# Projection split into halves on POOL, the second half of w2 staged through SP, and smaller landing margins in the planner of a fused hash-attention and maxout-FFN kernel

## The chip, the core and the metric

The kernel runs on one core of a Trainium2 chip. The metric is the device time in microseconds. A core has these engines: PE (matmul), DVE (vector), ACT (activation), POOL (GpSimd) and SP, which here only issues DMAs. Each engine works through its own queue in order, and waits at an instruction until what that instruction needs has been signalled. Everything queued behind it waits too.

## The reference

```python
q_bits = (np.einsum('bhsd,dk->bhsk', q, proj) > 0)         # batch 4, heads 8, seq 768, dim 64; 6 bits
k_bits = (np.einsum('bhsd,dk->bhsk', k, proj) > 0)
mask = q_bucket[:, :, :, None] == k_bucket[:, :, None, :]  # bucket: the 6 bits as a number
scores = np.where(mask, scale * q @ k.T, -1e9)
attn = softmax(scores)                                      # over the keys
x = (attn @ v).transpose(0, 2, 1, 3).reshape(3072, 512)
h = np.maximum(np.maximum(x @ w1, x @ w2), x @ w3)          # 512 -> 768
out = h @ w_out                                             # 768 -> 512, float32
```

## The kernel before

**The data path.** The work goes by pairs of heads, written (b, pr): batch b of 4, pair pr of 4. For each pair q and k are loaded in float32 and split into two float16 halves, a high part (split_h, L266 on ACT or L268 on DVE) and a residual (split_r, L273 on DVE). Both halves lie beside each other in a tile `s`. It is transposed into the operand tile `T`, by PE matmuls (L292) and copies (evac_T, L202 on ACT or L204 on DVE) for the first six pairs, and by a transposing DMA on SP (xbar, L282) for the others. `hash_mm` (L310, L312) multiplies T by the projection, which is held in the tile `PAB` as a float16 high part and a residual, both times 1024. The sign of the sum gives the bits (hash_bits, L330 and L332). The bits then replace the residual rows of T, so that the score matmul (L395) adds a large number for each bit that agrees, and the exponential (L401 on ACT) of anything else is zero. For the first pair the bits are written into `s` and transposed again. For all others they are transposed (bps, L339), copied (bt, L344), written to DRAM by SP (bit_out, L349, `dr<-bt`) and read back into T by SP (bit_in, L352, `T<-dr`). This is called the bounce below.

A unit is one score group (two L395 matmuls), one exponential on ACT and one attend group (six L413 matmuls). 192 units make the attention, six to a block; a block is normalized on DVE (L430, L436, L449). For rows whose bucket is empty the mean of v is added: from batch 1 on POOL sums v over its chunks (vsum, L363, L365, L366) and PE multiplies the sum by ones (mean_mm, L376, tile `svp`). In batch 0 PE does it from `vone` alone (L373).

The FFN takes half a batch of rows at a time: L478 matmuls by w1, w2 and w3, maxima on DVE (L487), L496 matmuls by w_out, copies and stores. Its float16 weights stay on chip. Each of w1, w2 and w3 comes in two halves of columns, named (half, i) with i = 0, 1, 2. By default a half is one DMA from POOL that converts on the way (`load_w`, L541). The halves in `plain`, and w_out ("o"), go another way: SP loads them in float32 in pieces (`stage_w`, L663) into one of two buffers `ws`, and POOL casts each piece (`cast_w`, L204).

**The order.** Nothing runs in program order of the loops. Every step is a task with the engines that may take it and their durations, a priority, dependences and buffers to take and give. `Plan.run` simulates the engines and a single queue of transfers (`xfer`), picks by priority what is free to start, and emits each instruction in that order into the engine queues. A DMA counts as landed when its transfer has passed that queue, plus POST = 1.2, plus the task's own `pad`: the landing margin. The queues of the hardware are fixed by this; a wait there costs what it costs. PE gets small filler matmuls (L771) until the first score, when it has nothing else.

The lines that the change touches: `make_p` (L231 to L239) and its task `mp` (L536) build PAB from `p32`. The key of the PSUM bank of `hash_mm` (L300, L315, L328) carries no head. The pads stand at the xbar task (L620) and at bit_in (L630). `plain` (L649) holds one half:

```python
    mp = add(("DVE", 0.5), -300, [add(("ACT", 0.1), -500, [], lambda e: None, lat=3.2)], make_p)
    ...
    plain = ((1, 2),)
    ...
    stage = {(0, 3): [(1, 0), (1, 1)], (1, 0): [(1, 2)], (1, 1): ["o"]}
```

`stage` says after which pair's bounce the weights are fetched: (1, 0) and (1, 1) after that of (0,3), (1, 2) after that of (1,0).

Of the kernel before, what the change touches and what calls it, by code (L numbers as in the profile page):

```python
# [10 lines left out]
AluOp = mybir.AluOpType  # L11
# [16 lines left out]
class Plan:  # L28
# [12 lines left out]
    def add(self, kinds, prio, deps, emit, **kw):  # L41
        t = Task(kinds if isinstance(kinds, list) else [kinds], prio, deps, emit, **kw)
        self.tasks.append(t)
        return t
# [89 lines left out]
def kernel(  # L134
# [12 lines left out]
    nc = tc.nc  # L147
    B, H, S, D = q.shape
    NBITS = proj.shape[1]
# [9 lines left out]
    NA = 4 * NCH  # L159
# [27 lines left out]
    op = ctx.enter_context(tc.tile_pool(name="op", bufs=OSB))  # L187
# [9 lines left out]
    add = plan.add  # L197
# [33 lines left out]
    def make_p(e):  # L231
        ph = konst.tile([D, NBITS], FP16, name="ph")
        pr32 = konst.tile([D, NBITS], FP32, name="pr32")
        nc.vector.tensor_copy(ph[:], p32[:])
        nc.vector.tensor_tensor(out=pr32[:], in0=p32[:], in1=ph[:], op=AluOp.subtract)
        for o in (0, D):
            for i, src in enumerate((ph, pr32)):
                nc.vector.tensor_scalar(out=PAB[o : o + D, NBITS * i : NBITS * (i + 1)], in0=src[:],
                                        scalar1=1024.0, scalar2=None, op0=AluOp.mult)  # L239


# [39 lines left out]
    def xbar(b, pr, e):  # L281
        nc.sync.dma_start_transpose(operand(b, pr)[:], S16[b, pr][:].rearrange("p a d -> p (a d)"))  # L282

    def bank(key, name):
        pss[key] = mm_ps.tile([P, 512], FP32, tag="mm", name=name)
        return pss[key]
# [10 lines left out]
        copy(e, operand(b, pr)[:, a0:a1, :].rearrange("p a t -> p (a t)"), p16[:, 0 : NCH * P])  # L297

    def hash_mm(b, pr, heads, e):
        hps = bank(("h", b, pr), "hps")  # L300
        summed = 4 * b + pr < 2
        K = NBITS if summed else 2 * NBITS
        for n in range(2):
            for hh in range(*heads):
                for c in range(NCH):
                    a = n * NA2 + hh * NCH + c
                    o = hps[:, a * K : (a + 1) * K]
                    if summed:
                        for i in range(2):
                            nc.tensor.matmul(o, T[b, pr][:, a, :], PAB[:, i * K : (i + 1) * K], start=i == 0, stop=i == 1)  # L310
                    else:
                        nc.tensor.matmul(o, T[b, pr][:, a, :], PAB[:], start=True, stop=True)  # L312

    def hash_bits0(pr, heads, e):
        hv = pss.pop(("h", 0, pr))[:, 0 : NA * NBITS].rearrange("p (n a k) -> p n a k", n=2, k=NBITS)  # L315
        sl = slice(heads[0] * NCH, heads[1] * NCH)
        bit = small.tile([P, 2, NA2, NBITS], FP16, tag="bit", name="bit")
        if pr:
            bits[0, pr] = bit
            nc.vector.tensor_scalar(out=bit[:], in0=hv, scalar1=0.0, scalar2=None, op0=AluOp.is_gt)  # L320
            return
        nc.vector.tensor_scalar(out=bit[:, :, sl, :], in0=hv[:, :, sl, :], scalar1=0.0, scalar2=0.5,  # L322
                                op0=AluOp.is_gt, op1=AluOp.subtract)
        nc.vector.tensor_scalar(out=S16[0, pr][:].rearrange("p (n a) d -> p n a d", n=2)[:, :, sl, D : D + NBITS],
                                in0=bit[:, :, sl, :], scalar1=2 * BIT, scalar2=None, op0=AluOp.mult)

    def hash_bits(b, pr, e):
        hv = pss.pop(("h", b, pr))[:, 0 : NA * 2 * NBITS].rearrange("p (a k) -> p a k", k=2 * NBITS)  # L328
        neg = small.tile([P, NA, NBITS], FP32, tag="neg", name="neg")
        nc.vector.tensor_scalar(out=neg[:], in0=hv[:, :, NBITS : 2 * NBITS], scalar1=-1.0, scalar2=None, op0=AluOp.mult)  # L330
        bits[b, pr] = bit = small.tile([P, 2, NA2, NBITS], FP16, tag="bit", name="bit")
        nc.vector.tensor_tensor(out=bit[:].rearrange("p n a k -> p (n a) k"), in0=hv[:, :, 0:NBITS], in1=neg[:],  # L332
                                op=AluOp.is_gt)
# [17 lines left out]
    def bit_in(b, pr, e):  # L351
        nc.sync.dma_start(T[b, pr][D : D + NBITS, :, :],  # L352
                          drs.pop((b, pr))[:].rearrange("n (a k) t -> k (n a) t", k=NBITS))
# [178 lines left out]
    for i, (n, pr, heads) in enumerate(order):  # L532
        half = heads != (0, 2)
        loads[n, 0, pr, heads] = add(("SP", 0.45), -400 + i, [], lambda e, n=n, pr=pr, heads=heads: load(n, 0, pr, heads, e),
                                     take=(n,) if heads[0] == 0 else (), xfer=0.55 if half else 1.1)
    mp = add(("DVE", 0.5), -300, [add(("ACT", 0.1), -500, [], lambda e: None, lat=3.2)], make_p)  # L536

    def load_w(i, half, e):
        w_ap = (moe_w1, moe_w2, moe_w3)[i].rearrange("(c p) f -> p c f", p=P)
# [21 lines left out]
    def prep(b, pr):  # L561
# [55 lines left out]
                                  give=("mm",)))  # L617
            both_rs += rs
        if not by_pe:
            ev = [add(("SP", 0.6), p0 + 2, both_rs, lambda e: xbar(b, pr, e), pad=4, xfer=4.6, hold=3.4, take=("T",))]  # L620
            xbars[4 * b + pr] = ev[0]
        plan.join(ev, ("s",))
        hm = add(("PE", 1.3 if 4 * b + pr < 2 else 0.67), p0 + 4, ev + [mp], lambda e: hash_mm(b, pr, (0, 2), e), take=("mm",))
# [3 lines left out]
        be = add(("DVE", 0.28), p0 + 6, [bT], lambda e: bit_evac(b, pr, e), take=("bt",), give=("mm",))  # L627
        bo = add(("SP", 0.65), p0 + 7, [be], lambda e: bit_out(b, pr, e), take=("dr",), give=("bt",), xfer=0.05,
                 after=[last_copy[0]])
        bi = add(("SP", 0.65), p0 + 7, [bo], lambda e: bit_in(b, pr, e), give=("dr",), xfer=0.25, pad=3 if 4 * b + pr > 5 else 0.0)  # L630
        bounced[b, pr] = last_copy[0] = bi
        if b == 0 and pr < NP - 1:
            for hh in range(2):
# [12 lines left out]
        t = small.tile([P, 1], FP16, tag="hold", name="hold")  # L646
        nc.gpsimd.tensor_copy(t[D : D + NBITS, :], T[b, pr][D : D + NBITS, NA - 1, P - 1 : P])

    plain = ((1, 2),)  # L649
    wst_tiles = {}  # L650

    def w_view(w, i):
# [153 lines left out]
```

The softmax here doesn't subtract the row's maximum and nothing guards it: scores larger than these inputs give would overflow.

## Time and profile before

| | before |
|---|---|
| median of 5 runs | 267.32 us (266.16 to 268.58) |
| profiled execution, its own time | 266.16 us |
| its span, first to last instruction | 264.4 us |
| PE busy | 255.6 us (97%) |
| ACT busy | 196.3 us (74%) |
| DVE busy | 174.7 us (66%) |
| POOL busy | 41.9 us (16%) |
| granted PE clock | 0.999 |

The profile holds one execution. Its times are microseconds from the start of the span; the 1.8 us between span and own time lie around it. "Busy" counts an instruction from start to end, also where matmuls overlap. Of the page, the slices show where in the span an engine worked, the chain shows what released each step of the work that ended last. In a timeline a line gives start, length, engine, source line, operation, tiles, and in brackets how long the engine had stood idle and what ended that. "SPq" and "POOLq" lines are the issue of DMAs, not the transfers.

### The profile page before, as it was taken

What the parts mean: (1) busy time and instruction counts of PE and PEld (TensorE: products, weight loads), DVE (VectorE), ACT (ScalarE), POOL (GpSimd) and SP (SyncE); (2) the same over time, 40 slices, a digit from 0 to 9 for tenths busy, and PEclk for the clock granted to TensorE, in tenths of its full rate; (3) what the DMA queues carried; (4) which work ended last, traced back from release to release, by engine and by line L of the source; (5) the groups of instructions that cost most, each with busy time, mean ns of one, the idle gap of its engine ahead of it and who ended that gap; (6) DMA issues with size and microseconds to landing.
All of it is one profiled execution on the core that took longest, in us unless ns stands there. A gap on an engine that the chain in (4) does not pass through costs nothing.

```text
span 264.4 us, 7323 instructions
## 1 busy us (share of the span) xinstructions
PE 255.6 (97%) x2992; PEld 174.0 (66%) x2992; DVE 174.7 (66%) x394; ACT 196.3 (74%) x283; POOL 41.9 (16%) x57
## 2 busy tenths in 40 slices
PE   7898899999999999999999999999999999999995
PEld 7787677767656666676666767766666656555552
DVE  4899589999748898468985795561655526255260
ACT  4799799997936889989899889989898632332322
POOL 1431054273311223003330030000000000000000
PEclk9999999999999999999999999999999999999999
DMA  6995489799997999979994995302030060120303
GB/s 206 342 277 90 135 265 267 228 230 338 218 224 253 241 255 171 236 210 207 211 246 140 219 179 103 71 14 109 12 62 0 4 179 4 40 79 0 121 0 120
DMA packets 67408, 41.69 MB, mean 158 GB/s; under 512 B 48046, under 2 KB 63662, under 8 KB 67374
## 3 DMA queue, kind: packets, MB, share of 16 engines
q1 hardware_dynamic: 64654, 39.26, 57.8%
q0 software_dynamic: 2640, 1.97, 4.8%
q8 instruction: 23, 0.38, 0.6%
q14 instruction: 11, 0.09, 0.1%
q10 hardware_dynamic: 80, 0.00, 0.0%
HBM read 25.72 MB, written 6.84 MB: 123 GB/s over the span
## 4 chain that ended last, share of the span: by engine, by line
PE 87%; ACT 5%; DMA 3%; DVE 3%; issue 1%; SPq 1%; ACTq 0%
PE ps L478 35%; PE sc L395 22%; PE av L413 12%; PE po L496 11%; ACT AT L401 4%; PE hps L312 3%; DMA q<-in_q_dram 2%; PE tps L292 1%; DMA T<-dr 1%; DVE s L268 1%; DVE s L273 1%; PE hps L310 1%; SPq L250 1%; PE bps L339 1%; ACT T L202 1%
## 5 line engine op out<-in xcount | busy, mean ns | idle before, releaser
L401 ACT ACTIVATE AT<-sc 128x768 f16<-128x768 f32 x192 | 146.2, 815 | 15.0 <-PE sc L395 12.9
L478 PE MATMUL ps<-xT,w_sb 128*128 128x384 f16 x576 | 106.3, 326 | 0.0
L395 PE MATMUL sc<-T 128*128 128x384 f16 x384 | 93.0, 325 | 2.6 <-DMA T<-dr 1.6
L487 DVE TENSOR_TENSOR ht<-ht,ps 128x384 f16<-128x384 f16 x96 | 52.9, 552 | 47.1 <-PE ps L478 44.6
L413 PEld LDWEIGHTS <-AT 128*128 128x128 f16 x1152 | 59.5, 97 | 22.6
L478 PEld LDWEIGHTS <-w_sb 128*128 128x128 f16 x576 | 52.6, 98 | 30.1
L413 PE MATMUL av<-vone,AT 128*128 128x65 f16 x1152 | 65.5, 193 | 0.0
L395 PEld LDWEIGHTS <-T 128*128 128x128 f16 x384 | 30.2, 97 | 13.2 <-DMA T<-dr 1.8
L496 PE MATMUL po<-wout_sb,ht 128*128 128x512 f16 (+1 forms) x150 | 33.6, 370 | 0.0
L202 ACT CAST ht<-ps 128x384 f16<-128x384 f32 x28 | 13.5, 480 | 26.4 <-DVE ht L487 19.1
L202 ACT COPY osb<-po 128x512 f32<-128x512 f32 (+1 forms) x24 | 13.7, 569 | 18.3 <-PE po L496 18.3
L363 POOL TENSOR_TENSOR vt<-v 128x384 f32<-128x384 f32 x12 | 13.6, 1134 | 66.4 <-DMA v<-in_v_dram 66.3
L430 DVE TENSOR_TENSOR t<-av,mv 128x390 f32<-128x390 f32 x32 | 18.0, 561 | 8.1 <-PE av L413 8.0
L496 PEld LDWEIGHTS <-ht 128*128 128x128 f16 x150 | 14.1, 98 | 13.7
L273 DVE SCALAR_TENSOR_TENSOR s<-q,s 128x384 f16<-128x384 f32 x32 | 20.2, 646 | 3.3 <-ACT s L266 3.2
L449 DVE TENSOR_TENSOR xn<-t,rr 128x384 f16<-128x384 f32 x32 | 18.7, 583 | 1.1
L273 DVE SCALAR_TENSOR_TENSOR s<-k,s 128x384 f16<-128x384 f32 x32 | 17.7, 574 | 0.4 <-ACT s L266 0.2
L204 DVE CAST ht<-ps 128x384 f16<-128x384 f32 x20 | 11.1, 556 | 10.1 <-PE ps L478 9.7
L292 PE MATMUL tps<-iden,s 128*128 128x128 f16 x168 | 13.3, 219 | 1.8 <-DVE bit L322 1.1
L292 PEld LDWEIGHTS <-s 128*128 128x128 f16 x168 | 10.3, 97 | 3.3 <-DVE s L273 2.2
L312 PEld LDWEIGHTS <-T 128*128 128x128 f16 x336 | 10.0, 96 | 1.0
L312 PE MATMUL hps<-PAB,T 128*128 128x12 f16 x336 | 10.4, 168 | 0.0
(54 smaller groups left out, 141.7 us busy)
## 6 DMA issues: line engine op xcount, KB each, us to landing
v<-in_v_dram SPq DMA_DIRECT2D x16, 384.0 KB
out_dram<-osb SPq DMA_DIRECT2D x23, 256.0 KB
q<-in_q_dram SPq DMA_DIRECT2D x15, 384.0 KB
k<-in_k_dram SPq DMA_DIRECT2D x15, 384.0 KB
w_sb<-in_moe_w_dram POOLq DMA_DIRECT2D x5, 384.0 KB, 10.9
ws<-in_moe_w_out_dram SPq DMA_DIRECT2D x3, 512.0 KB
ws<-in_moe_w_dram SPq DMA_DIRECT2D x2, 384.0 KB
dr<-bt SPq DMA_DIRECT2D x15, 36.0 KB
```

Of the source, the lines that this page charges most:

```text
L202: nc.scalar.copy(o, i)
L273: nc.vector.scalar_tensor_tensor(out=s[:, a0:a1, D : 2 * D], in0=raw_view(n, b, pr, heads), scalar=QS, in1=s[:, a0:a1, 0:D], op0=AluOp.mul ...
L292: nc.tensor.transpose(p16[:, c * P : (c + 1) * P], S16[b, pr][:, a0 + c, :], iden[:])
L312: nc.tensor.matmul(o, T[b, pr][:, a, :], PAB[:], start=True, stop=True)
L395: nc.tensor.matmul(sc[:, i, 0:HQ], t[:, NA2 + hh * NCH + 2 * j + i, :], t[:, hh * NCH + hf * CH : hh * NCH + (hf + 1) * CH, :], start=True ...
L401: nc.scalar.activation(AT[:], scs.pop(u)[:, :, 0:HQ], ActFn.Exp, bias=EXP_BIAS, scale=EXP_SCALE)
L413: nc.tensor.matmul(av[:, o : o + D + 1], AT[:, i, c * P : (c + 1) * P], vones[b % 2][:, 2 * pr + hh, 2 * j + i, 0 : D + 1], start=slot == ...
L430: nc.vector.tensor_tensor(out=t[:, :, :, 0 : D + 1], in0=av[:, :, :, 0 : D + 1], in1=mv, op=AluOp.add)
L449: nc.vector.tensor_tensor(out=xv, in0=t[:, :, :, 0:D], in1=rr[:].to_broadcast([P, 2, CH, D]), op=AluOp.mult)
L478: nc.tensor.matmul(ps[:, 0:HQ], w_sb[i][:, jc, fb * P : (fb + 1) * P], xTs[b, hf][:, jc, :], start=jc == 0, stop=jc == NJ - 1)
L487: nc.vector.tensor_tensor(out=ht[:], in0=ht[:], in1=ps[:, 0:HQ], op=AluOp.max)
L496: nc.tensor.matmul(ps[:, m0:m1], hts[b, hf, fb][:, c * P : (c + 1) * P], wout_sb[:, fb, m0:m1], start=fb == 0, stop=fb == NF - 1)
```

## The change

Four edits. `make_p` issues its six instructions on POOL, and its task is planned there with 1.5 in place of 0.5. The PSUM bank of the hash gets the first head into its key, so that the two heads of pair (0,0) may be in flight in two banks. The pads of xbar and bit_in are one unit smaller. The half (1, 1), the second half of w2, joins `plain`: SP loads it in two pieces and POOL casts them, where one POOL DMA did it before. As the planner lays out all queues from these numbers, the order on every engine changes.

```diff
     def make_p(e):
         ph = konst.tile([D, NBITS], FP16, name="ph")
         pr32 = konst.tile([D, NBITS], FP32, name="pr32")
-        nc.vector.tensor_copy(ph[:], p32[:])
-        nc.vector.tensor_tensor(out=pr32[:], in0=p32[:], in1=ph[:], op=AluOp.subtract)
+        nc.gpsimd.tensor_copy(ph[:], p32[:])
+        nc.gpsimd.tensor_tensor(out=pr32[:], in0=p32[:], in1=ph[:], op=AluOp.subtract)
         for o in (0, D):
             for i, src in enumerate((ph, pr32)):
-                nc.vector.tensor_scalar(out=PAB[o : o + D, NBITS * i : NBITS * (i + 1)], in0=src[:],
+                nc.gpsimd.tensor_scalar(out=PAB[o : o + D, NBITS * i : NBITS * (i + 1)], in0=src[:],
                                         scalar1=1024.0, scalar2=None, op0=AluOp.mult)
...
-        hps = bank(("h", b, pr), "hps")
+        hps = bank(("h", b, pr, heads[0]), "hps")
...
-        hv = pss.pop(("h", 0, pr))[:, 0 : NA * NBITS].rearrange("p (n a k) -> p n a k", n=2, k=NBITS)
+        hv = pss.pop(("h", 0, pr, heads[0]))[:, 0 : NA * NBITS].rearrange("p (n a k) -> p n a k", n=2, k=NBITS)
...
-        hv = pss.pop(("h", b, pr))[:, 0 : NA * 2 * NBITS].rearrange("p (a k) -> p a k", k=2 * NBITS)
+        hv = pss.pop(("h", b, pr, 0))[:, 0 : NA * 2 * NBITS].rearrange("p (a k) -> p a k", k=2 * NBITS)
...
-    mp = add(("DVE", 0.5), -300, [add(("ACT", 0.1), -500, [], lambda e: None, lat=3.2)], make_p)
+    mp = add(("POOL", 1.5), -300, [add(("ACT", 0.1), -500, [], lambda e: None, lat=3.2)], make_p)
...
-            ev = [add(("SP", 0.6), p0 + 2, both_rs, lambda e: xbar(b, pr, e), pad=4, xfer=4.6, hold=3.4, take=("T",))]
+            ev = [add(("SP", 0.6), p0 + 2, both_rs, lambda e: xbar(b, pr, e), pad=3, xfer=4.6, hold=3.4, take=("T",))]
...
-        bi = add(("SP", 0.65), p0 + 7, [bo], lambda e: bit_in(b, pr, e), give=("dr",), xfer=0.25, pad=3 if 4 * b + pr > 5 else 0.0)
+        bi = add(("SP", 0.65), p0 + 7, [bo], lambda e: bit_in(b, pr, e), give=("dr",), xfer=0.25, pad=2 if 4 * b + pr > 5 else 0.0)
...
-    plain = ((1, 2),)
+    plain = ((1, 1), (1, 2))
```

## The prediction

> **What bounds the kernel now.** I read the page first: engine totals and the 40 slices, then the chain that ended last, then the timelines of SP, POOL and PE around the stretches that the change touches.
>
> ```profile
> PE 255.6 (97%) x2992; PEld 174.0 (66%) x2992; DVE 174.7 (66%) x394; ACT 196.3 (74%) x283; POOL 41.9 (16%) x57
> PE   7898899999999999999999999999999999999995
> PE 87%; ACT 5%; DMA 3%; DVE 3%; issue 1%; SPq 1%; ACTq 0%
> ```
>
> PE is busy 97% of the span, and the chain is PE for 87% of it. The Trainium skill, "Perfetto Trace Analysis", Identifying the Most-Contended Engine, warns that matmul busy time says little because matmuls are pipelined. So I counted work: four L478 matmuls follow each other in 0.65 us, two L395 in 0.33, six L413 in 0.185. Summed over all groups this is about 249 us of a 264.4 us span. Some 13 us of the rest lie before 48.6 us, about 3 are the last copy and store. From 48.6 on the chain is almost only PE, back to back. Hence two rules for this kernel: work taken off DVE or ACT after 48.6 us is worth nothing, and **any wait that PE's own queue meets there is lost whole**, since no idle time is left later to take it up.
>
> The start has one gate that everything before it runs into (chain of waits, start and length in us):
>
> ```profile
> 24.30 0.71 ACT AT L401
> 25.02 2.41 DMA T<-dr
> 27.48 0.82 PE sc L395 x4
> ```
>
> The bits of head pair (0,1) go through DRAM. Their read is issued at 25.02 and lands at 27.48; PE stood 1.63 us, ACT 2.11. From there to the first FFN matmul at 48.59, ACT sets the pace (10.00 and 9.97 of 10 us busy in the windows from 30 and 40). Then comes a place with almost no slack (timelines of SP, POOL, PE; start, length, engine, line):
>
> ```profile
> 41.48 0.32 SPq L349 DMA_DIRECT2D dr<-bt  x1
> 47.08 0.29 SPq L352 DMA_DIRECT2D T<-dr  x1
> 47.41 0.91 SPq L663 DMA_DIRECT2D ws<-in_moe_w_dram  x2
> 51.08 0.82 POOL L204 CAST w_sb<-ws 128x768 f16<-128x768 f32 x1 [7.74 <-DMA ws<-in_moe_w_dram]
> 52.24 1.23 POOL L204 CAST w_sb<-ws 128x768 f16<-128x768 f32 x1 [0.34 <-DMA ws<-in_moe_w_dram]
> 53.43 1.32 POOL L363 TENSOR_TENSOR vt<-v 128x384 f32<-128x384 f32 x1
> 55.37 0.65 POOL L366 TENSOR_TENSOR vsum<-vt,vt 128x128 f16<-128x128 f32 x1
> 55.98 1.32 POOL L363 TENSOR_TENSOR vt<-v 128x384 f32<-128x384 f32 x1
> 56.43 0.22 PE L376 MATMUL svp<-vsum,ones 128*128 128x130 f16 x1
> ```
>
> The write of the bits of pair (1,0) is issued at 41.48, and only when it has landed, at 47.08, can SP issue their read and the two staged pieces of w3. POOL casts those, then sums v of pair (1,2), done at 56.02. PE's mean matmul that needs this sum starts at 56.43: 0.41 us of slack.
>
> **What the Trainium skill says here.** "GPSIMD Engine Reference", 3.1, gives a two-input add on GpSimd 1.96 times the VectorE time and about 156 ns of dispatch. The trace agrees: L363 on POOL takes 1134 ns for 128x384, L430 on DVE 561 ns for 128x390; the small copy "hold" takes 184 ns on POOL, the projection's copy 158 ns on DVE. "DMA: Bandwidth & Descriptors", Queues, rings and completion order, says that each DMA engine alternates between the queues that have work, packet by packet, and that a semaphore lands only after the engine's earlier writes. The trace agrees in kind: weight loads from POOL's queue need 9.8 to 12.5 us to land while SP's queue is full, and the write issued at 41.48 took 5.6 us, against 2.36 us for the one at 25.39, when DMA was nearly idle.
>
> **The change part by part.** The planner rewrites all queues; I use the order in which the built new program lists them.
>
> *Projection on POOL.* Six DVE instructions of 0.16 us (4.16 to 4.97) go. On POOL I price them at 6 x 0.2 = 1.2 us (hold 0.18; bounds 6 x 0.15 and 6 x 0.5 us). POOL is idle from 1.3 to 10.32, where v arrives. The projection, issued at 0.74, is there by 4.16 at the latest, so PAB is ready between 4.3 and 7.2. In the new order the first hash matmul needs PAB only after both operand copies of the first head. The second of them stands on DVE behind the fourth split_r, which ran at 7.20 and waits for data, so hash starts near 8.4 (before: 6.89). Cost 0. The DVE time set free gains nothing at once: the next split waits for a q load that landed at 5.33.
>
> *The new start order.* Both heads of pair (0,0) go through hashing before the first score. By walking the queues with the durations above, the first score moves from 12.04 to about 12.7, the first exp from 12.56 to about 13.5. After it come 12 exps at 0.75, 3 copies at 0.75 and one split of 0.84: ACT is through at about 26. All of this lies in front of the gate at 27.48, so it costs 0 (about 1.5 us of cover). The write of (0,1) is ready at about 19.5 (before 19.90), but the DMA engines are over-full until 22, so I leave the gate where it is.
>
> *Gate to FFN.* Both orders have 23 exps there. Before: 3 copies of T and one v cast (0.72 each) on ACT; after: 2, the cast and one small xT copy (0.38). ACT saves 0.34. The work of PE up to the first FFN matmul is equal within 0.1 us. FFN starts at about 48.2: **-0.4 us**.
>
> *Second half of w2 through SP and POOL casts.* One POOL DMA of 0.75 us issue goes, two SP issues of 0.45 us and two POOL casts of 1.0 us come. SP: the two loads stand before q, k, v of pair (1,2) and before the write of the bits of (1,0). At 310 GB/s (window from 34 to 36) each 384 KB take 1.27 us, so that write has 2.5 us more ahead of it in SP's queue, and the same bytes less beside it in POOL's. It is issued about 1.3 us earlier, which does not help behind the loads. Bounds for its landing: 0 (all bytes done at the same time) and +2.0 us; I take **+1.0**, to 48.1. The loads of q and k of (1,2) also come two places later, near 45.8 and 47.1; DVE wants q at about 46.5, ahead of the last xT copy before the FFN, and k at about 48.6. I take 0, and up to +0.5 if q is late. The transpose of (1,2) on SP, issued at 53.95 before, needs DVE's last split near 53.4: unchanged.
>
> *POOL's queue.* Before: sum (1,1), casts of w3, sum (1,2). After: four casts, then sum (1,1), then (1,2). So the sum of (1,1) now waits for w3's pieces, which wait for that landing. Same durations: first sum done at 56.02 + 1.0 = 57.0, second at 58.4 + 1.0 = 59.4. PE, from 48.2: 6 L478 groups 3.90 + 8 score pairs 2.64 + 8 attend groups 1.48 + 0.12 = 8.14, so it is at the first mean matmul at 56.3 and waits 0.7. After 1.74 us more it is at the second and waits 0.6. All matmuls of scores, attention and FFN are queued behind: **+1.4 us** with 0.1 for the wake-ups. With bounds 0 and +2.0 for the landing: +0.4 and +2.5. The later sum of (1,3), now behind two w_out casts, is done near 68.1, when PE in this case is there at 68.9: 0.
>
> *Smaller margins.* No instruction goes. The transposed operands' hash matmuls came 6.3 to 8.5 us after SP had issued the transpose; with one unit less planned they keep 5 or more. First scores came at least 4.2 us after the issue of T<-dr, and landing took 2.5. I take +0.1; bounds 0 and +1.5. A gain is excluded, since PE has other work there.
>
> Sum: -0.4 + 1.4 + 0.1 = **+1.1 us**, 267.3 us of span and outside work on the profiled execution (266.16 us, span 264.4). That execution is the fastest of the five shown; set on their median of 267.32 it gives **268.4**.
>
> **The rivals.**
> 1. *Slower.* The landing at 47.08 moves by the full 2.0 us: the mean matmuls then wait 2.5, and one or two operand waits of the smaller margins add 0.5 to 1: +2.6 to +3.2, about 270.2. It decides from a landing later than about 48.4. For it: the slack of 0.41 us. Against: total bytes are equal.
> 2. *No wait.* The write lands as before or earlier. Only the 0.4 us of FFN start remain, less up to 0.4: 266.9 to 267.3. Then the shift of weights and margins does nothing that can be seen. For it: DMA is equally full up to 46.5.
> 3. *Faster.* The earlier write of (0,1) lands earlier, and the gate gives back most of the 1.63 us PE stood there, with 0.4 at FFN: about 265.6. For it: DMA carried 86 GB/s and less from 22 on. Against: full queues until 22.
>
> **How the numbers follow.** Forecast case 0.45 (own range 267.3 to 269.1), slower 0.27, no wait 0.18, faster 0.10. What this kernel's measurement can tell from no change is about 0.5%, 1.34 us. The forecast lies inside; a quarter of its case passes the bound upwards. Slower: 0.27 + 0.11 = 0.38; faster: 0.10 + 0.02 = 0.12; same 0.50. Range 266.2 to 270.6, with one in ten left out on each side.
>
> **What would show it.** Right: T<-dr near 48, POOL's casts of w3 near 52, and in the waits "PE svp L376 <- POOL vsum" of 1 to 1.5 us, first FFN matmul near 48.2. Wrong: no such wait; a T<-dr of (0,1) away from 25.0; PE waits on T after 60 us (margins too small), or a first hash that waits for PAB.

## The result and the profile after

| | before | after |
|---|---|---|
| median, same chip | 268.09 us (265.58 to 271.42, 80 runs) | 268.41 us (265.90 to 272.96, 43 runs) |
| ratio after to before | | 1.0014 [0.9998, 1.003] |
| profiled execution, own time | 266.16 us | 269.06 us |
| its span | 264.4 us | 267.3 us |

Every ratio here, with its interval, is formed from the fast runs of both kernels alone (a run over 1.5% above its kernel's fastest counts as slow), so it need not be the quotient of the two medians beside it. In this comparison nothing happened that the measurement can tell from no change; the interval ends at 0.3%. By the two profiles the change cost 2.9 us. So the first thing to learn is that one profiled execution is a draw: that of before was one of the fastest of 80, that of after stood 0.65 us above its median. A second profile of each was therefore taken (below).

The page of the changed kernel, totals, PE's 40 slices and the chain by engine:

```profile
PE 255.1 (95%) x2986; PEld 173.7 (65%) x2986; DVE 169.1 (63%) x380; ACT 199.6 (75%) x291; POOL 45.3 (17%) x64
PE   7799889989899999999999999999999999999994
PE 72%; ACT 9%; DMA 8%; DVE 3%; POOL 3%; issue 2%; SPq 1%; ACTq 0%; POOLq 0%
```

PE does the same work within 0.5 us. Two slices behind 48 us (the ninth and the eleventh) fell from 9 to 8, and in the chain PE gave 15 points away, most of them to DMA, ACT and POOL. Two of the waits of PE in this kernel (what waited and for whom: us in total, times, longest):

```profile
PE svp L376 <- POOL vsum L366: 2.4, 3, 1.3
PE sc L395 <- DMA T<-dr: 1.2, 1, 1.2
```

The first line is the wait that the prediction named; the second is the gate. The timeline of SP's queue shows where the first comes from:

```profile
40.14 0.32 SPq L349 DMA_DIRECT2D dr<-bt  x1
48.61 0.29 SPq L352 DMA_DIRECT2D T<-dr  x1
49.00 1.53 SPq L663 DMA_DIRECT2D ws<-in_moe_w_dram  x2
...
53.25 7.12 SPq L282 DMA_TRANSPOSE T<-s  x1
```

The write of the bits of (1,0) goes out 1.34 us earlier than before and its landing comes 1.5 us later, as the read behind it shows. The transposing DMA of (1,2) is issued at 53.25 and then holds SP for 7.12 us, which means that nothing behind it in SP's queue is issued in that time. Before it was 3.78 us:

```profile
53.95 3.78 SPq L282 DMA_TRANSPOSE T<-s  x1
```

POOL and PE of the changed kernel, in their timelines (in brackets the idle time and what ended it):

```profile
52.87 1.85 POOL L204 CAST w_sb<-ws 128x768 f16<-128x768 f32 x2 [7.58 <-DMA ws<-in_moe_w_dram]
...
56.32 0.46 POOL L366 TENSOR_TENSOR vsum<-vt,vt 128x128 f16<-128x128 f32 x1
...
58.56 0.46 POOL L366 TENSOR_TENSOR vsum<-vt,vt 128x128 f16<-128x128 f32 x1
65.23 1.04 POOL L204 CAST wout_sb<-ws 128x1024 f16<-128x1024 f32 x1 [6.21 <-DMA ws<-in_moe_w_out_dram]
...
69.40 0.65 POOL L366 TENSOR_TENSOR vsum<-vt,vt 128x128 f16<-128x128 f32 x1
```

```profile
47.90 0.81 PE L478 MATMUL ps<-xT,w_sb 128*128 128x384 f16 x4
...
56.83 0.22 PE L376 MATMUL svp<-vsum,ones 128*128 128x130 f16 x1 [0.69 <-POOL vsum L366]
59.07 0.22 PE L376 MATMUL svp<-vsum,ones 128*128 128x130 f16 x1 [0.36 <-POOL vsum L366]
70.11 0.22 PE L376 MATMUL svp<-vsum,ones 128*128 128x130 f16 x1 [1.31 <-POOL vsum L366]
```

The casts of w3 start when DMA delivers, the sums of (1,1) and (1,2) follow at once, and PE waits 0.69 and 0.36 us. Later the casts of w_out start late too, and PE waits 1.31 us for the sum of (1,3).

**An account that fits.** From the traces I took three numbers of each execution: when the first FFN matmul starts, how long PE stands idle from there to 156 us, and the rest. The idle time is read from windows like these two, of before and of after (length, then busy time with instructions in brackets for PE, PEld, DVE, ACT and POOL, PE's granted clock, DMA share, GB/s): 107.41 less 107.26, and 108.10 less 105.23.

```profile
48.59:156.00 107.41, 107.26 (x1292) 72.21 (x1289) 85.42 (x188) 92.19 (x131) 28.36 (x35) 1.00 0.96 231
47.90:156.00 108.10, 105.23 (x1265) 70.61 (x1262) 80.73 (x182) 93.09 (x135) 31.53 (x38) 1.00 0.95 228
```

| execution | own time | first FFN matmul | PE idle after it | rest |
|---|---|---|---|---|
| before | 266.16 | 48.59 | 0.15 | 217.4 |
| before, second profile | 268.20 | 48.47 | 1.69 | 218.0 |
| after | 269.06 | 47.90 | 2.87 | 218.3 |
| after, second profile | 268.67 | 47.05 | 3.53 | 218.1 |
| after, sums first | 267.74 | 46.70 | 2.75 | 218.3 |
| after, no staging of w2 | 268.21 | 47.81 | 2.28 | 218.1 |

The rest is own time less the other two: PE's work from the FFN start on, the last stores, and the 1.8 us outside the span. It is constant within 0.9 us, which is as much as the effects at stake. In all six executions PE had done the same scores (74 of its L395 matmuls) and ACT the same 36 exponentials before the first FFN matmul, so the starts can be compared. A gain then shows as an earlier FFN start, a loss as idle time behind it, and the changed kernel has both. This is an account of where the time lies in six single executions; it does not yet say what causes the idle time.

### The profile page after: what moved, and what is told of

It is laid out like the page before. It is cut to its first block, busy times and chain, and to the rows that moved or that the text cites. A ratio compares the mean times of both kernels' runs of the same rounds, so it can differ in the third digit from the quotient of the medians.

```text
span 267.3 us, 7322 instructions
## 1 busy us (share of the span) xinstructions
PE 255.1 (95%) x2986; PEld 173.7 (65%) x2986; DVE 169.1 (63%) x380; ACT 199.6 (75%) x291; POOL 45.3 (17%) x64
## 3 DMA queue, kind: packets, MB, share of 16 engines
q1 hardware_dynamic: 65198, 40.04, 57.5%
q0 software_dynamic: 2112, 1.57, 3.8%
HBM read 25.72 MB, written 6.84 MB: 122 GB/s over the span
## 4 chain that ended last, share of the span: by engine, by line
PE 72%; ACT 9%; DMA 8%; DVE 3%; POOL 3%; issue 2%; SPq 1%; ACTq 0%; POOLq 0%
PE ps L478 32%; PE sc L395 16%; PE po L496 12%; PE av L413 9%; ACT AT L401 7%; DMA q<-in_q_dram 2%; DMA dr<-bt 2%; DMA ws<-in_moe_w_out_dram 2%; PE hps L312 2%; DMA ws<-in_moe_w_dram 1%; DVE s L273 1%; ACT T L202 1%; DMA T<-dr 1%; ACT s L266 1%; POOL vt L363 1%
## 5 line engine op out<-in xcount | busy, mean ns | idle before, releaser
L478 PE MATMUL ps<-xT,w_sb 128*128 128x384 f16 x576 | 106.7, 326 | 0.0
L395 PE MATMUL sc<-T 128*128 128x384 f16 x384 | 93.2, 325 | 2.4 <-DMA T<-dr 1.2
L478 PEld LDWEIGHTS <-w_sb 128*128 128x128 f16 x576 | 51.9, 98 | 31.3 <-issue 2.6
L395 PEld LDWEIGHTS <-T 128*128 128x128 f16 x384 | 30.6, 97 | 13.9 <-issue 1.6
L202 ACT CAST ht<-ps 128x384 f16<-128x384 f32 x33 | 15.9, 482 | 27.7 <-DVE ht L487 20.6
L273 DVE SCALAR_TENSOR_TENSOR s<-q,s 128x384 f16<-128x384 f32 x32 | 19.1, 612 | 4.6 <-ACT s L266 4.5
L204 DVE CAST ht<-ps 128x384 f16<-128x384 f32 x15 | 8.3, 556 | 14.9 <-PE ps L478 14.8
L292 PE MATMUL tps<-iden,s 128*128 128x128 f16 x168 | 13.5, 219 | 2.4 <-DVE s L273 1.3
L292 PEld LDWEIGHTS <-s 128*128 128x128 f16 x168 | 10.5, 98 | 3.7 <-DVE s L273 2.7
## 6 DMA issues: line engine op xcount, KB each, us to landing
w_sb<-in_moe_w_dram POOLq DMA_DIRECT2D x4, 384.0 KB, 10.6
```

Source lines behind the costliest of these rows:

```text
L202: nc.scalar.copy(o, i)
L273: nc.vector.scalar_tensor_tensor(out=s[:, a0:a1, D : 2 * D], in0=raw_view(n, b, pr, heads), scalar=QS, in1=s[:, a0:a1, 0:D], op0=AluOp.mul ...
L292: nc.tensor.transpose(p16[:, c * P : (c + 1) * P], S16[b, pr][:, a0 + c, :], iden[:])
L395: nc.tensor.matmul(sc[:, i, 0:HQ], t[:, NA2 + hh * NCH + 2 * j + i, :], t[:, hh * NCH + hf * CH : hh * NCH + (hf + 1) * CH, :], start=True ...
L478: nc.tensor.matmul(ps[:, 0:HQ], w_sb[i][:, jc, fb * P : (fb + 1) * P], xTs[b, hf][:, jc, :], start=jc == 0, stop=jc == NJ - 1)
```

## The experiments

**1. The kernel before, profiled again.** No edit.

> The kernel before, unchanged, for a second profile. Its times run over 5 us, and the profile shown is near the low end of them. Theory (the same late landings occur in before): a profiled execution of 267 to 269 us with PE waits of 0.5 to 2 us after 48 us, for a POOL sum or an operand. Rival: the span differs by a general slowness, with no PE wait after 48 us.

268.20 us. Two of the waits that it loses time to, from PE's timeline:

```profile
56.86 0.22 PE L376 MATMUL svp<-vsum,ones 128*128 128x130 f16 x1 [0.39 <-POOL vsum L366]
87.41 0.48 PE L395 MATMUL sc<-T 128*128 128x384 f16 x2 [0.61 <-ACT AT L401]
```

The spot where the prediction read 0.41 us of slack has a wait of 0.39 us in this execution. T<-dr of (1,0) came at 47.65 here and at 47.08 there. So waits of PE behind 48 us occur in the kernel before too, in one of its two profiles; the first had nearly none. How often they occur, two executions can't say.

**2. Sums first.** In both kernels only POOL's queue is changed. In the changed kernel the sums of (1,1) and (1,2) go ahead of the casts of w3, and the sum of (1,3) ahead of the first two casts of w_out; in the kernel before the sum of (1,2) goes ahead of the casts of w3. The edit, with the names and comments of this text:

```diff
+    # (w, i): the pair whose sum goes ahead of this cast; before has the first two alone
+    DEFER = {((1, 2), 0): (1, 2), ((1, 2), 1): (1, 2), ("o", 0): (1, 3), ("o", 1): (1, 3)}
     def cast_w(w, i, e):
-        copy(e, w_view(w, i)[1], wst_tiles.pop((w, i)))
+        late.setdefault(DEFER[w, i], []).append((w, i)) if (w, i) in DEFER else copy(e, w_view(w, i)[1], wst_tiles.pop((w, i)))
+    flush = lambda key: [copy("POOL", w_view(w, i)[1], wst_tiles.pop((w, i))) for w, i in late.pop(key, [])]
+    # at the end of vsum(b, pr): flush((b, pr))
```

> The changed kernel with POOL's queue alone reordered: the sums of v of (1,1) and (1,2) stand ahead of the casts of w3, that of (1,3) ahead of the first two casts of w_out; every other queue is the same. Theory (the mean matmuls that wait for POOL are the loss): the three waits PE svp <- POOL vsum, 2.4 us in the changed kernel's profile, go, no other PE wait takes their place, and the time falls by 1.4 to 2.4 us, to about 266.3, ratio to before 0.991 to 0.997. Rival (PE would meet the next late thing anyway, the w_out casts or an operand): the waits move, the time stays within 0.5 us of 268.4.

> The kernel before with POOL's queue alone reordered: the sum of v of (1,2) ahead of the casts of w3. Theory (the 0.41 us of slack of its mean matmul is used up in ordinary executions, and the profile shown of before was a lucky one): 0.3 to 1.2 us faster than before, ratio 0.995 to 0.999. Rival (before has no such wait in most executions): no change, 0.999 to 1.001.

The changed kernel: 267.68 us, ratio to before 1.0009 [0.997, 1.0048]. The kernel before: 267.51 us, 1.0035 [0.9997, 1.0072]. The waits for sums are gone from the changed kernel's list, and others stand in their place:

```profile
PE av L413 <- DVE t L430: 1.9, 3, 0.8
PE po L496 <- POOL wout_sb L204: 0.6, 1, 0.6
```

PE stands idle for 2.75 us behind the FFN start, against 2.87 and 3.53 in the changed kernel: what the sums had cost is taken by the next late things. One is DVE's normalization. The other is the cast of the third piece of w_out, which this edit does not move: SP could issue that piece only at 69.42, behind the transpose of (1,3), which had held it for 7.61 us. No gain can be told from none, and the fall of 1.4 to 2.4 us that the theory expected did not come; a gain of up to 0.8 us against before lies within the interval. The one profile of the kernel before with sums first took 270.47 us, the longest of its 14 runs, and is not read for waits.

**3. With and without the staging of w2.** Once the changed kernel without it, once the kernel before with it alone (and the head in the bank's key).

```diff
# in the changed kernel
-    plain = ((1, 1), (1, 2))
+    plain = ((1, 2),)
# in the kernel before
-    plain = ((1, 2),)
+    plain = ((1, 1), (1, 2))
```

> The changed kernel with the second half of w2 loaded by one POOL DMA as before; the projection on POOL, the bank keys and the smaller margins stay. Theory (the two staged loads ahead of the bits of (1,0) delay them): the read T<-dr of (1,0) is issued near 47.1 again instead of 48.6, PE's waits for POOL sums are below 0.5 us, time about 267.0 to 267.6, ratio 0.996 to 0.998. Rival (smaller margins or the new start order cost the time): waits of PE elsewhere, ratio 1.001 to 1.006.

> The kernel before with only the second half of w2 staged through SP and cast on POOL (the planner then puts the casts of w2 ahead of the sum of (1,1), the casts of w3 behind it; the head in the bank's key is kept too). The prediction's step says that the two loads ahead of the write of the bits of (1,0) make it land 1.0 us later (0 to 2.0). Theory A: the issue of T<-dr of (1,0) comes 15.6 to 16.6 us after that of (0,3), against 14.4, 15.6 and 14.8 in three executions without the staging; the sum of (1,1) is on time, the sum of (1,2) is done 1 us later than in before, near 57 to 58, PE waits 0.7 to 1.5 us there once, and the median is 0.4 to 1.2 us above before. SP's transpose of (1,2) ends 10.5 to 11.8 us after T<-dr of (1,0), as in all executions so far, whenever it was issued. Rival B (equal bytes, no delay): distance of at most 15.2 us, no wait above 0.5, median within 0.4 us of before.

The change without staging: 268.21 us, ratio to before 1.0005 [0.9963, 1.0048]. The staging alone: 269.11 us, 1.0035 [1.0009, 1.0061], so +0.9 us (0.0035 x 268.1). In the change without staging the theory's steps came as expected: T<-dr of (1,0) is issued at 46.98, and sums cost PE 0.2 us, not 2.4. The time did not: PE waits for exponentials instead, 1.17 us at 139.88 and 0.54 us at 73.50, and stands 2.28 us in all. So in the changed kernel the waits for sums go when the staging goes, but that gains nothing that can be told from none. POOL's new order is not the staging's: without it the sum of (1,1) still stands behind the casts of w3, and with the staging alone it stands ahead of them.

The landing is compared by the distance between two issues on SP, T<-dr of (0,3) and T<-dr of (1,0), which leaves out how early the start was: with staging 16.32, 16.26 (the changed kernel twice), 15.60 (sums first), 15.40 (old margins, below) and 15.89 us (alone), mean 15.9; without it 14.41, 15.56 and 14.78 us, mean 14.9. On these means the bits land 1.0 us later with the staging, but single executions overlap, and the one profile of the kernel before with sums first, which has no staging, has 15.87.

With the staging alone that delay is not where the time went: PE waits 0.3 us for sums in that profile, since the planner leaves the sum of (1,1) ahead of the casts of w3. It starts the FFN at 49.04, stands 0.84 us behind it, and its rest is 219.05, 1 us more than in the table. Its PE queue is laid out differently behind the start; what this microsecond is stays open.

**4. More bytes ahead of the write.** The kernel before with 768 KB more in SP's queue. They copy v within DRAM, and nobody reads the copies. The edit, written out in short:

```diff
     def load(n, b, pr, heads, e):
...
         ENG[e].dma_start(raws[n, b, pr][:, h0:h1, :], ...)
+        if (n, b, pr) == ("v", 1, 2):
+            for i in range(2):
+                nc.sync.dma_start(spare[i], v[1, 2 * i : 2 * i + 2])   # spare: DRAM
```

> The kernel before with two more DMAs in SP's queue, behind the load of v of pair (1,2) and ahead of the write of the bits of (1,1) and the transpose of (1,2): each copies 393 KB of v from DRAM to a spare place in DRAM that nobody reads. It asks what sets how long the transposing DMA holds SP: 3.8 to 7.1 us in the executions so far. Theory A (SP is held until the transfers queued ahead are through, so the end follows the bytes and not the issue): the transpose is issued at 53.3 to 55 as before, and ends 12.5 to 14 us after T<-dr of (1,0), against 10.5 to 10.9 without the extra bytes (786 KB at 250 to 310 GB/s are 2.5 to 3.1 us); the hold is 6 to 7.5 us. T<-dr of (1,1) and the pieces of w_out follow 2 to 3 us later, the sum of (1,3) is done at 71.5 to 73 and PE waits for it 1 to 3 us. Rival B (the hold belongs to the transpose itself, 3.7 us, and grows with traffic beside it): it ends at most 11.5 us after T<-dr of (1,0).

The expectation misplaces the edit: v of (1,2) is loaded near 36 us, so the bytes went ahead of the write of the bits of (1,0), and the sum near 70 us is that of (2,0). So this run does not test what it was written for, but it measures the disputed step directly. SP's timeline, and PE's:

```profile
36.69 2.21 SPq L243 DMA_DIRECT2D m<-in_v_dram  x2
41.27 0.34 SPq L349 DMA_DIRECT2D dr<-bt  x1
50.60 0.27 SPq L352 DMA_DIRECT2D T<-dr  x1
...
54.08 6.25 SPq L282 DMA_TRANSPOSE T<-s  x1
```

```profile
59.32 0.22 PE L376 MATMUL svp<-vsum,ones 128*128 128x130 f16 x1 [2.94 <-POOL vsum L366]
```

T<-dr of (1,0) comes 2.95 us later than in the second profile of before (50.60 against 47.65), which is 768 KB at 267 GB/s: in this one execution the write of 36 KB came later by about the time of all bytes that were put ahead of it. PE then stands 2.94 us at the mean matmul, and the execution takes 272.14 us, 3.2 us over the median of before beside it. So the slower rival's mechanism is real: a late landing goes over into PE's wait nearly whole. Its size is not tested, since the rival spoke of 2.0 us. That the change stays below it because its 768 KB ahead replace bytes beside is the prediction's reason, and fits, but no run shows it.

**5. The changed kernel, profiled again.** No edit.

> The changed kernel as it is, with a second profile. It asks which of the waits in the first one come back and which belong to that execution. Theory A (the waits for POOL's sums are the change's own): T<-dr of (1,0) is issued 15.6 to 16.6 us after that of (0,3), PE waits at the mean matmuls behind the casts of w3 for 0.5 to 1.5 us in all, and the transpose of (1,2) ends 10 to 12 us after T<-dr of (1,0); if T<-dr comes at 48 or earlier, SP is held for 5.5 us or less and the sum of (1,3) is done before 69.5, with a wait of at most 0.7 us. Median 267.7 to 269.3. Rival B (the first profile was an ordinary one, wait for wait): the sum of (1,3) comes after 69.9 again and PE waits over 1 us for it. Rival C (the waits were chance): no wait for a sum above 0.3 us.

268.74 us, ratio to before 1.0036 [1.001, 1.0063]; profiled at 268.67. In this comparison the interval lies above 1: a loss of 0.3 to 1.7 us. The first expectation holds in kind, but with 2.7 us of waits, not at most 1.5, and with SP held for 6.13 us, not at most 5.5. SP's queue, then PE's:

```profile
47.53 0.29 SPq L352 DMA_DIRECT2D T<-dr  x1
...
52.41 6.13 SPq L282 DMA_TRANSPOSE T<-s  x1
```

```profile
57.16 0.22 PE L376 MATMUL svp<-vsum,ones 128*128 128x130 f16 x1 [1.87 <-POOL vsum L366]
59.91 0.22 PE L376 MATMUL svp<-vsum,ones 128*128 128x130 f16 x1 [0.86 <-POOL vsum L366]
```

The FFN starts at 47.05, 0.85 us earlier than in the first profile, and PE waits 1.68 us more at these two matmuls. PE is through with the second at 60.13 here and at 59.29 there, whatever the start had won. The landing is not what makes these waits: T<-dr of (1,0) came at 47.53, and at 47.65 in the second profile of before. The second piece of w3 came at nearly the same time in both as well. Its cast, here and then in the second profile of before:

```profile
53.89 0.83 POOL L204 CAST w_sb<-ws 128x768 f16<-128x768 f32 x1 [1.91 <-DMA ws<-in_moe_w_dram]
53.53 0.83 POOL L204 CAST w_sb<-ws 128x768 f16<-128x768 f32 x1 [0.66 <-DMA ws<-in_moe_w_dram]
```

What differs is that PE comes earlier, and that the sum of (1,1) now stands behind this cast, where in that profile of before it had been done at 43.96. The third wait, for the sum of (1,3), is gone: that sum is done at 67.97, and the prediction had said 68.1.

**6. The changed kernel with the old margins.** Up to about 65 us all queues are the same.

```diff
-            ev = [add(("SP", 0.6), p0 + 2, both_rs, lambda e: xbar(b, pr, e), pad=3, ...
+            ev = [add(("SP", 0.6), p0 + 2, both_rs, lambda e: xbar(b, pr, e), pad=4, ...
-        bi = add(("SP", 0.65), p0 + 7, [bo], lambda e: bit_in(b, pr, e), ..., pad=2 if 4 * b + pr > 5 else 0.0)
+        bi = add(("SP", 0.65), p0 + 7, [bo], lambda e: bit_in(b, pr, e), ..., pad=3 if 4 * b + pr > 5 else 0.0)
```

> The changed kernel with the old landing margins (4 and 3 in place of 3 and 2). The order of every engine is the same up to about 65 us and differs behind it. It asks what the smaller margins alone do. Theory A (the prediction's step: +0.1 for the change, bounds 0 and +1.5): median within 0.7 us of the changed kernel beside it, same waits before 65 us, no PE wait on a T in either. Rival B (the smaller margins make PE wait on operands after 65 us): this kernel is 0.7 to 1.5 us faster, and waits of hps or sc on T that the changed kernel shows are gone. Rival C (the margins are what keeps the changed kernel level with before, in spite of the staging): this kernel is 0.7 to 1.5 us slower.

269.64 us (6 runs), ratio to before 1.0105 [1.0051, 1.0159], beside 1.0036 [1.001, 1.0063] of the changed kernel in the same session. The old margins look 0.9 us slower, as the third rival has it; the intervals overlap, so it is likely, not settled. The one large wait that this profile has and the changed kernel's two have not:

```profile
75.96 0.82 PE L478 MATMUL ps<-xT,w_sb 128*128 128x384 f16 x4 [1.39 <-DMA xT<-xn]
```

An FFN group stands there ahead of the landing of its xT, in an order that the planner built on other landing times. But PE's idle time from the FFN start to 156 us is 3.60 us in all, against 3.53 in the second profile of the changed kernel, so this wait does not explain the 0.9 us; that stays open. Behind the gate no wait of a score or hash matmul for a landing T came or went.

**7. The weight loads out of the way of the gate.** The kernel before; POOL issues the first halves of w1, w2 and w3 later. First behind its fourth cast of v, then behind a small copy that waits until T<-dr of (0,1) has landed.

```diff
-        nc.gpsimd.dma_start(w_sb[i][:, :, f], w_ap[:, :, f])
+        (wl.append if half == 0 else lambda x: x())(lambda: nc.gpsimd.dma_start(w_sb[i][:, :, f], w_ap[:, :, f]))
+        # first run: all of wl is called at the end of vcast(0, 3)
+        # second run: in bit_in(0, 1): hold(0, 1, e), then all of wl
```

> The kernel before, with one queue changed: POOL issues the three loads of the first halves of w1, w2 and w3 after its cast of v for pair (0,3), the fourth, instead of after the first cast. All other queues stand as they are. It asks what holds the start: in the kernel before, T<-dr of pair (0,1) is issued at 24.6 to 25.0 and lands 2.4 us later, while DMA is full until 22 us and nearly idle after. Theory A (the 2.36 MB of weights, at about 310 GB/s some 7.6 us of all engines, delay q, k, v and then the write of the bits of (0,1)): v of (0,3) arrives near 14 to 16 instead of 20, the loads then begin only there, and the T<-dr of (0,1) is issued at 21.5 to 23.5. PE's idle time before 28 us falls by 1 to 1.6 us, the first FFN matmul comes at 47 to 47.5, and the median is 0.8 to 1.6 us below that of before. Rival B (the write of the bits is late because its own producers are late, or because the moved loads now stand beside it): T<-dr of (0,1) within 0.5 us of 24.8 and the median within 0.6 us of before. Rival C (the gate opens earlier, but the gain is taken by the later waits after 48 us, which an ordinary execution of before also has: 0.4 at the mean matmul and 1.1 at 84 to 96): T<-dr of (0,1) early, first FFN matmul early, and still a median within 0.6 us.

> As the run with late weight loads, but POOL holds the three loads of the first halves of w1, w2, w3 until T<-dr of pair (0,1) has landed (one more small hold copy on POOL, 0.2 us). So no weight byte moves before the gate. Theory A: the write of (0,1) meets no other traffic and takes 2.3 to 2.5 us instead of 4 to 5; it is issued near 19 to 20, T<-dr near 21.5 to 22.5, landing near 24.5; PE's idle time before 28 us goes down to what the split and bit work leaves (at most 0.5), ACT sets the pace from 24.5, first FFN matmul at 46 to 47. The weights land by 38, ahead of their use. Median 1.2 to 2.0 us below before. Rival B (producers set the write): write issued at 20 or later, T<-dr at 22.5 to 23, gain under 0.6. Rival C: gate early by 2 us, but the loads now collide with q, k, v of batch 1 at 27 to 36, and the bits of (1,0) or the mean matmul at 56 give the gain back: waits of PE after 48 us grow by 1 us or more and the median is within 0.6 of before.

271.17 us, 1.0111 [1.0077, 1.0146], and 271.87 us, 1.0141 [1.0104, 1.0178]. In the second the gate opened as wanted and the next bounces paid. Its SP queue:

```profile
19.98 0.37 SPq L349 DMA_DIRECT2D dr<-bt  x1
21.55 0.28 SPq L352 DMA_DIRECT2D T<-dr  x1
...
28.65 0.32 SPq L349 DMA_DIRECT2D dr<-bt  x1
37.01 0.29 SPq L352 DMA_DIRECT2D T<-dr  x1
```

The write of (0,1) took 1.6 us without weights in its way, against 3.9 and 5.1 in the two profiles of before: the loads do set the gate. PE was busy 3.94 of 4 us from 24 to 28. But the loads then lay ahead of the write of (0,3), which took 8.4 us in place of 1.7 to 1.8, and beside T<-dr of (0,2), which landed 5.5 us after its issue; PE stood 1.58 us for that, and 2.05 us for a late copy of T at 43.84. In the first run they lay ahead of T<-dr of (0,1) itself, and PE stood 3.69 us there. Rival C had expected the gain to be given back, not a loss of 3 us. Part of the excess is PE's clock (windows of the run with the loads behind the gate, columns as in the account above; the clock is the third figure from the end, 0.60 and 0.54):

```profile
32.00:36.00 4.00, 2.73 (x24) 1.81 (x23) 2.23 (x5) 2.90 (x4) 0.00 (x0) 0.60 1.19 239
36.00:40.00 4.00, 4.00 (x41) 3.09 (x40) 2.80 (x7) 2.54 (x5) 0.12 (x1) 0.54 0.47 132
```

**8. The gate without DMA.** The bits of (0,1) take the path of (0,0): into `s`, and transposed again by PE, with four more copies on ACT or DVE. Once on the kernel before, once on the changed one.

```diff
-        if pr:                       # in hash_bits0: the bits of (0,1) kept apart
...
+        if (b, pr) == (0, 1):        # after hb, in place of bT, be, bo and bi
+            for hh in range(2):
...
+                for n in "qk":
+                    t = add(("PE", 0.5), p0 + 6, [hb], lambda e, n=n, hh=hh: pe_T(n, 0, 1, hh, e), take=("mm",), ...)
+                    ready_T[b, pr, hh].append(add(both(0.52, 0.8), p0 + 7, [t], lambda e, n=n, hh=hh: evac_T(n, 0, 1, hh, e), ...))
...
+            return
```

> The kernel before, with the bits of pair (0,1) on the path that pair (0,0) has: written into s on DVE and transposed again by PE (12 more groups of transposes in four banks, four more copies of T on ACT or DVE), in place of the way through DRAM. The planner lays out the queues anew; the next write to DRAM is that of (0,2). It asks what the gate at 27.48 is worth when no DMA stands in it and no byte is moved into another bounce's way, which the two runs with late weight loads did. Cost: PE 2 us of transposes and ACT or DVE 4 x 0.75 us, in a stretch where PE stands 1.2 to 1.8 us and ACT 1 to 2 us. Theory A (the gate is worth its idle time): T of (0,1) is complete at 22 to 24, PE has no idle stretch over 0.5 us between 24 and 28, first FFN matmul at 46.5 to 47.5, and the median is 0.5 to 1.5 us below before. Rival B (ACT or DVE becomes the bound: the four copies push the splits of (0,2) and (0,3), whose bounces then come late and PE waits there instead): first FFN matmul within 0.5 us of 48.5 and the median within 0.7 us of before. Rival C (what is won at the start is lost to the landing of the bits of (1,0) or to the sums on POOL, which do not come earlier): FFN early, waits after 48 us above 2 us, median within 0.7 us.

> The changed kernel with the same edit for the bits of pair (0,1). Theory A: 0.5 to 1.5 us below the changed kernel's 268.4, that is 267 to 267.9; the sum of (1,1) still waits behind the casts of w3, so a wait of 0.5 to 1.5 us at PE's mean matmul stays. Rivals as for the same edit on before; if the sums take the gain, the median is 268 to 269 and the waits for POOL's sums are above 2 us.

On the kernel before: 270.83 us beside 268.94 of before, 1.0102 [1.0042, 1.0162]. On the changed kernel: 274.51 us, 1.0206 [1.0142, 1.0271]. In the first the gate is gone: PE 4.00 of 4 us busy from 24 to 28, first FFN matmul at 46.69, 1.8 us earlier than in the second profile of before. Still its profiled execution, the fastest of its six, took 268.09 us: one unit of attention fewer had been done by then (35 exponentials, not 36), and PE stood 2.25 us behind the FFN start, not 1.69, the longest at

```profile
74.46 0.59 PE L492 MATMUL po<-wout_sb,ht 128*128 128x512 f16 x2 [0.80 <-POOL wout_sb L204]
```

The pieces of w_out do not come earlier because PE does: SP issued the third at 68.56 here and at 68.81 in the second profile of before. On the changed kernel the mean matmul at 46.52 waited 1.92 us for a sum, and the FFN started at 50.66. In kind this is rival C, at a higher price: the losses are 2.7 and 5.5 us (0.0102 and 0.0206 x 268.1), and what the other executions lost is not in the profile of the fastest, so it stays open. None of these versions is faster than either kernel.

## Why the prediction came out right, point by point

- **Sum and range.** Predicted 268.4, measured 268.41 in the comparison and 268.74 beside the second profile. The sum of +1.1 us stands against +0.4 [-0.1, +0.8] and +1.0 [+0.3, +1.7] us (ratios less 1, times 268.1): the second fits, by the first it was too large. That the absolute time was met to 0.01 us is luck: the median it was set on, 267.32 of five runs, became 268.09 with 80, 0.8 us higher, and by the medians the change cost 0.3 us in place of 1.1, 0.8 us less. And terms of the sum were off in opposite directions, as the next points show.
- **Projection on POOL, cost 0.** Six instructions from 3.46 to 5.55, 2.1 us in place of 1.2 (the page of waits shows no hash matmul that waits for PAB). The four multiplications took 0.23 to 0.48 us each, on DVE 0.16 to 0.17. Right, mis-sized where it costs nothing.
- **New start order.** First score at 13.09 and first exponential at 13.68, predicted 12.7 and 13.5; both in front of the gate. Right.
- **Gate to FFN, -0.4 us: too small.** The changed order started the FFN at 47.90 and 47.05, before at 48.59 and 48.47: -1.1 us on the mean. The prediction left the gate at 25.0; T<-dr of (0,1) came at 24.85 and 23.58, and in the run with sums first at 23.66. So a part of the *faster* rival was true in some executions, and its gain was lost behind the FFN start. The earlier start goes with the projection on POOL and the order planned around it: it stays without the staging (47.81) and with the old margins (47.44), and it is missing where staging and bank key come without it (49.04). Each of these is one execution, and the move alone was not run.
- **Landing of (1,0), +1.0 us: right as a delay, not as a time.** The distances of experiment 3 give 1.0, and experiment 4 gives the price of bytes ahead without the relief of bytes taken away beside: 2.95 us for the same 768 KB. But the start came earlier by about as much, so that T<-dr was issued at 48.61 and 47.53, for 48.1 predicted, and at 47.08 and 47.65 before. The relief was also set too high. What the prediction calls "the same bytes less beside it" holds for what is read from DRAM (25.72 MB in both pages); as the pages count the queues, POOL's gave up 0.40 MB (1.97 to 1.57) and SP's took 0.78 (39.26 to 40.04).
- **Sums at 57.0 and 59.4: right, by the named path in the first profile alone.** They were done at 56.78 and 59.02, then at 57.11 and 59.85. In the second profile the landing was early and the second piece of w3 late (experiment 5). The waits of +1.4 us were 1.05 and 2.73 us: PE came earlier than predicted, and the sums did not. That such a wait "is lost whole" was right as bookkeeping, but to remove it (experiments 2 and 3) gave nothing back that can be seen, since others took its place.
- **Sum of (1,3), cost 0: the term that was mis-sized.** It was done at 70.05 in the first profile, not 68.1, and cost 1.31 us; at 67.97 in the second, and cost 0. The step took the issue of the transpose of (1,2) as unchanged at 53.95, and let its hold of SP be unchanged with it. It was issued at 53.25 in the first profile, but held SP for 7.12 us, and T<-dr of (1,1) and the w_out loads stood behind. In the table below, twelve executions have its end 9.7 to 11.8 us behind T<-dr of (1,0), whenever the transpose was issued; in the thirteenth it was issued only after 10.2 us, and then held SP for the shortest time.
- **Margins, +0.1 and no gain possible: doubtful.** Experiment 6 speaks for a gain of 0.9 us. The reason given, that PE has other work, missed that the pads also decide the order, and with it which other waits arise.
- **Against the first profile.** From 266.16 to 269.06 is +2.9 us. Of the excess, 1.5 us is the wait that before has in its second profile and not in its first (1.69 against 0.15).

| | issued after T<-dr of (1,0) | hold of SP | end after T<-dr of (1,0) |
|---|---|---|---|
| extra bytes ahead of the write | 3.48 | 6.25 | 9.7 |
| after | 4.64 | 7.12 | 11.8 |
| after, second profile | 4.88 | 6.13 | 11.0 |
| late weight loads | 5.38 | 5.26 | 10.6 |
| before, second profile | 5.71 | 4.75 | 10.5 |
| staging alone | 5.99 | 4.51 | 10.5 |
| after, sums first | 6.06 | 4.75 | 10.8 |
| after, old margins | 6.14 | 4.73 | 10.9 |
| loads behind the gate | 6.37 | 4.53 | 10.9 |
| before, bits of (0,1) by PE | 6.52 | 4.36 | 10.9 |
| after, no staging | 6.84 | 3.78 | 10.6 |
| before | 6.87 | 3.78 | 10.7 |
| after, bits of (0,1) by PE | 10.18 | 3.74 | 13.9 |

That SP is held until the five loads issued between T<-dr and the transpose are through is what these numbers suggest; no run took those loads away, so it is not shown. The Trainium skill, "DMA: Bandwidth & Descriptors", Queues, rings and completion order, says that a DMA's signal comes only after the earlier writes of its engines. The write of 36 KB in experiment 4 agrees in kind (9.3 us from its issue to the read that waits for it).

## What to carry to other kernels

Where PE is the bound and DMA is full, an earlier start is worth only as much as the deliveries behind it can follow: here up to 1.8 us won before the FFN came back as idle time behind it, at one late result or another. Before moving bytes, look at which small latency-bound transfer stands behind them. Bytes ahead over the bandwidth are an estimate of its delay from above: here 768 KB put ahead went with 2.95 us where nothing was taken away, in one execution, and with about 1.0 us on the mean where bytes beside were. And take a second profile of the kernel before: a slack of 0.4 us read from one execution is no slack, and a difference of one profile from another is not the effect.

## What the runs showed of the hardware

- A transposing DMA of one size (T<-s) held SP's queue for 3.6 to 8.0 us over all profiles, and everything behind it in that queue with it. In the table above it was issued 3.5 to 6.9 us after T<-dr in twelve executions and ended 9.7 to 11.8 us after it: an earlier issue went into a longer hold.
- A write of 36 KB took 1.6 to 2.4 us from its issue to the read that waits for it where DMA was nearly idle, and 5.4 to 9.3 us, over all profiles, for that of (1,0), which has loads ahead of it.
- PE's granted clock fell after stretches with little PE work. Windows of the run with the weight loads behind the fourth cast of v, then of the run with more bytes ahead of the write, same columns as above:

```profile
24.00:28.00 4.00, 0.92 (x22) 0.79 (x19) 2.10 (x6) 1.06 (x2) 0.00 (x0) 1.00 1.11 176
28.00:32.00 4.00, 3.40 (x43) 2.46 (x44) 0.91 (x3) 1.53 (x3) 0.00 (x0) 0.57 0.39 123
```

```profile
56.00:60.00 4.00, 1.06 (x8) 0.50 (x5) 2.70 (x4) 1.91 (x3) 3.48 (x5) 0.96 1.13 306
60.00:64.00 4.00, 4.00 (x31) 2.44 (x30) 2.88 (x6) 1.61 (x3) 1.54 (x3) 0.62 1.02 238
```

  It fell to 0.57 after a wait of 3.69 us, and to 0.62 after one of 2.94. There the wait costs more than its own length: four L478 matmuls, 0.81 us at the full clock, took 1.22 and 1.49 us behind the wait of 2.94. The length of one wait does not decide it: in the second profile of the changed kernel the clock stayed at 1.00 through waits of 1.87 and 0.86 us, with PE busy for 1.98 of the 4 us from 56 to 60, while in the run with the loads behind the gate it fell to 0.60 from 32 us on after waits of 1.58 and 0.27 us, with PE busy for 2.38 of the 4 us from 28 to 32. What does decide it, these traces don't show. The Trainium skill, "TensorE: Matmul & The Clock Gate", Part 1: The HAM clock gate, tells of a gate that throttles after an idle window of about 3.4 us. The wait of 3.69 us agrees with that; in the other two falls PE had not been idle for so long.
